# Turning the x of batches 4 and 5, the residual of batch 3 and the q and k of batch 6 by transposing transfers in a fused attention and wave-MLP kernel

## The chip, the cores and the metric

The kernel runs on one core of one Trainium2 chip. The core has five engines that run their own instruction queues and meet at semaphores: TensorE (PE in the profile, its weight loads PEld), VectorE (DVE), ScalarE (ACT), GpSimd (POOL) and SyncE (SP), which here only issues transfers. The metric is the device time of one execution in microseconds (us); smaller is better.

## The reference

Two steps on inputs of batch 8, 8 heads, 576 rows and head size 64, all float32. First, attention: a coarse one over means of four rows, repeated to full length, plus a local one in which a row sees the rows less than 4 away. Then a wave-MLP on the result, x of 576 x 512 for each batch.

```python
q_d, k_d, v_d = means of four rows of q, k, v
out_up = np.repeat(sm_attn(q_d, k_d, v_d), 4, axis=2)
mask = np.abs(pos[:, None] - pos[None, :]) < 4
out_local = softmax(where(mask, q @ k.T / 8, -1e9)) @ v
x = out_up + out_local                      # to (B, S, H * D)
theta = x @ w_theta
y = w_tok_r @ (x * cos(theta)) + w_tok_i @ (x * sin(theta))
u = x + y
return u + np.maximum(u @ w_ch, 0.0)
```

## The kernel before

Everything is computed in bf16 with sums in float32. Each batch passes through the same chain of steps, each step a small function that emits the instructions of one piece. A step has a name of two letters:

- `lk`, `lq`, `lv`, `lw` load quarters of k and q and halves of v chunks into one of 14 staging buffers `st`; `ck`, `cq`, `cv` cast them to bf16 (on DVE, ACT or POOL, as a letter says).
- `tp` turns nine 128x128 squares of q or k on TensorE into PSUM and `ev` copies them out to `kT` or `qT`. For the batches in `QKD` a transposing transfer `dk` does the turn instead, into a staging buffer, and `ev` copies from there.
- `kd`, `qd` take the means; `ps`, `ex`, `mk`, `po`, `nm` are scores, exponentials, mask, product with v and normalisation of the local part; `sd`, `ed`, `nd`, `xn`, `xd`, `xc` are the same of the coarse part (`pv`, `vd` its v); `xt` turns the local result, and `xa` adds both into `xT` (x with channels on partitions).
- `th`, `cs` are theta and its cosine and sine for 128 rows, `tt`, `ct`, `zt` the same for the last 64 rows.
- `xm` turns 128 rows of x back on TensorE into PSUM, four squares, and `zz` on DVE multiplies them with cosine and sine into `z`. For the batches in `XDMA` four transposing transfers `dx`, one for each 128 channels, fill the one buffer `xx` instead, and `zz` reads that: each `zz` needs all four `dx`, and the next batch's `dx` need all four `zz`.
- `mx` (nine products of 288 columns) mixes over rows, `ua` adds x and gives `uT`.
- `up` turns 128 rows of u back on TensorE and `uc` copies them to `ur` (the residual). For batches not in `RPE` four transposing transfers `du` fill `ur`. `zp` and `dz` are the same pair for the last 64 rows of z.
- `ch` is the product with w_ch, `rl` on DVE takes the maximum with 0 and adds `ur`, `st` stores 128 rows. `ut`, `dt`, `ht`, `rt`, `ss`, `sr` do the last 64 rows of two batches together.

Batch 0's v takes another way (`l1`, `c1`, `t1`, `e1`, `x1`). `lc`, `cc`, `la`, `ca`, `lb`, `cb`, `wp`, `wc` bring in the weights. `te` and `ts` load a table on ACT, `wm` are products on zeros that keep TensorE busy at the start.

The order of all this is a table, `ORDER`: one word for each step, with the PSUM bank, staging buffer or engine behind the name. The function `pin` ties every instruction to the one before it on its engine, so each engine runs its part of the words strictly in their order, SP's transfers included. A transfer's issue waits on SP until its source and its target are free, and everything behind it on SP waits too. Eight banks of PSUM, 14 staging buffers and five output buffers are shared by all steps.

Of the kernel before, what the change touches and what calls it, by code (L numbers as in the profile page):

```python
# [57 lines left out]
la2 cqg lb1 tp45 qdv eva wm22 tp23 eva wm65 ps67 kdg vdv lq3 qdv ckg cka ps45 cag ex wm25 sd23 ex lb4 ed cbg lk5 sd01  # L60
cqg ps67 mkv ed po45 nm po23 nd45 nd01 la6 nm la7 xn xn lk8 mkg tp23 cag po45 ex xt6 po01 cqa eva la9 lqa mkg caa xd7
lqb ckg xca ckg nm tp23 nm xt4 xt5 lbd cag lbc cbg lb2 xt7 xa cqg lb1 eva lb0 cbg lb3 lb6 tp01 xa po23 th4 xa xm5 xa
lv7 cqg nm cbg th6 lw xt7 cbg th2 lv5 xm3 evv cbg ts cs tp01 lv8 lv9 cs cbg xa tt4 zz cs xm5 wp6 wp2 zz lw lw wp3 lw
lv4 lw cbg lqa zz ct lqd eva qdg ztv wp7 cba th4 wcv zp5 lkb xm6 wcv lkc kdg wcv wp2 wp3 wcv zcv wp0 wcv wp1 cs wp7
wca wcv ps45 lk2 lk1 wcv wcv ps23 te ex qdg ps01 lq0 zz kdv cva ex mx7 mx6 mx4 cvg ua sd23 cvg cvg mkv lc3 ex po01 ua
sd67 ed ed mkv mx5 ua nm po23 ua po01 cvg pv67 nm nm mkg vda mx4 ua po23 lq6 cqg po67 nd01 nm nd45 mx2 up3 xn lq7 ckg
xn cqg lk5 cka nm tp01 xd4 lk8 up5 uca eva xcv xt3 ucv lk9 tp67 cka xt4 xt0 ua ckg xt1 kdg lv4 xa xa xa mx5 xa eva lva
tp23 ua th4 xt0 lw xa evv cqg th5 xm1 lvb lcd lqc tt0 lw lk1 lv2 lv0 lw ts cs lw xm4 cqg cs tp67 ckg cqg th2 xm3 th5
ct lw cka zz tp01 cs qdg zz cs xm2 evv ztg lc6 lc5 zp4 mx6 ccg zz qdg zcv zz eva cvg mx7 ps45 te ex ua ps23 ua ckg kdv
ex mkv ps01 mx6 lq7 mx7 po45 sd23 ex lq8 lk3 kdg ed cvg sd01 cqg ckg ua lk4 lq9 mx6 tp23 mkv lva lw lvc lw nm ua tp45  # L70
up7 cvg mkv cvv ed mx0 eva cvg pv23 ccg ua ucv eva po67 po45 ua nm up1 nm vda ccg ccg ch0 nd67 lq1 xn nd23 lkb cqg cqa
tp45 uca qdg xn mx1 xd2 xt3 eva ps67 rl lq0 ua po45 xcv kdg qdg ps01 ch2 xa ckg ex mkg nm rl mx3 ps67 cqg lv2 cka po45
ex ua sd01 lkd xt2 ckg ex nm mx3 xt4 xt5 xa up2 ua cqa cqg tp67 cvv ed up3 xa evv uca th0 xa lv6 xt1 up2 xa lw th4 xm6
ucv ts cs uca th5 cvg lq5 ckg po01 cvg zz cs nm po23 xm7 cs ch6 nm tt4 tp01 lw ct tp23 th5 rl mkg ch4 lq7 zz st eva
evv rl po67 sd01 cs cqg cvg ztg po23 ch5 nm nm rl ch4 lv8 lw te ed cvg st pv67 vda zp0 zca lk4 cka lk3 lk1 tp23 cqa
mkg ckg lq9 lqb rl qdg lva lw xm1 eva ckg utg lv0 zz lw xm5 ch4 nd67 lvc zz xn lw nd01 mx5 lvd xn mx6 st ps23 rl lv2
ua po01 kdg nm ps45 ua mx7 lk5 ex xd0 cqa xt1 ex up6 ua xcv ucv lk6 kdv tp23 cqg utg mx0 tp45 qdg xa ua eva sd67 xt2
lv8 xt3 ch1 eva xa mkg ed xa th0 mkv rl cvg lk3 lw xt6 xt7 xa xa lw lk1 cvg th2 mx1 ua ts cs xm3 cvg tt0 zz th6 st lq4
cs cvg cka po45 dt cvg ckg ct po23 th7 mx1 ztg lk7 cs lvb nm pv45 cs ckg po67 cqg kdg lw nm ua sd23 mx0 cvg nm te ed
zp1 tp67 vdv zcv ht2 tp45 xm1 rt lw ua lq9 mx3 eva zz ps67 eva ua lva qdg po45 nm ex ps01 lq0 ex xm2 up3 zz lqc nd67  # L80
uca lvd tp45 cqa xm2 qdg xn nd01 zz mx3 cka cka xn mx2 xd0 up1 lk2 lv6 kdg st ua mx3 cqa mkv lw uca xcv eva tp67 xt0
up1 lk5 ua ua cva ucv xt4 xa mx5 st xa st eva ps23 mkg sd01 qdg po67 lw ed ua nm lv3 xt4 mx5 xt6 cva mx7 po01 ua ex
sd23 xa xa po45 lw nm cvg th6 nm lq4 cqv xt0 lw ed cvv xa ts cs tp23 mkv lv8 th1 cs xm4 ua ch5 kdg lw rl ch6 lv9 eva
tt0 th1 th7 xm5 pv23 utv ct ztg zz up0 ss cqg cs zz vdv mx1 uca ua xm0 lv1 lw st zz cs tp45 lv7 cvg lv0 cvg lqb nd23
xm7 ch1 eva kdg rl nd45 xn mx0 rl xn dz ch1 sr ps23 ps45 lw lw qdg lw te ex lka zz po67 ua mx0 ex ps23 cqa ex nm rl ua
# [12 lines left out]
"""


# [1 line left out]
def kernel(  # L102
# [489 lines left out]
    def zz(b, c, w):  # L592
        x = xx[:, c, :] if b in XDMA else at.pop(("xm", b, c))
        nc.vector.tensor_tensor(out=z[b % 2][:, 2 * c:2 * c + 2, :],  # L594
# [163 lines left out]
```

## Time and profile before

| what | value |
|---|---|
| median of 3 runs | 231.97 us (231.42 to 232.17) |
| span of the profiled execution, first to last instruction | 229.4 us |
| instructions | 8506 |
| TensorE clock granted, mean | 0.996 of full |
| packets and bytes moved | 76647, 49.35 MB |
| first scores of batch 0 start at | 18.84 us |

The profile gives the execution's span, and no time of that execution beyond it; the times of the runs are from other executions. Engines work beside each other, so the sum of their busy times says nothing; what sets the time is read from where the busiest engine waits and for whom. The prediction shows the lines.

### The profile page before, as it was taken

What the parts mean: (1) busy time and instruction counts of PE and PEld (TensorE: products, weight loads), DVE (VectorE), ACT (ScalarE), POOL (GpSimd) and SP (SyncE); (2) the same over time, 40 slices, a digit from 0 to 9 for tenths busy, and PEclk for the clock granted to TensorE, in tenths of its full rate; (3) what the DMA queues carried; (4) which work ended last, traced back from release to release, by engine and by line L of the source; (5) the groups of instructions that cost most, each with busy time, mean ns of one, the idle gap of its engine ahead of it and who ended that gap; (6) DMA issues with size and microseconds to landing.
All of it is one profiled execution on the core that took longest, in us unless ns stands there. A gap on an engine that the chain in (4) does not pass through costs nothing.

```text
span 229.4 us, 8506 instructions
## 1 busy us (share of the span) xinstructions
PE 219.7 (96%) x3491; PEld 154.2 (67%) x3491; DVE 185.6 (81%) x377; ACT 159.3 (69%) x239; POOL 144.1 (63%) x190
## 2 busy tenths in 40 slices
PE   7898899999999999999999999899999999999992
PEld 2455778696778765776788667676676665677740
DVE  5168999999899899797898969979898889476382
ACT  2389899759987899689887896779879258600000
POOL 7768999929999989991984456892697310200000
PEclk9999999999999999999999999999999999999998
DMA  6999999999989999999998007996576357376677
GB/s 181 387 391 391 268 190 222 374 271 226 235 270 249 248 345 177 231 261 233 291 220 211 21 17 191 302 214 126 136 132 187 68 118 206 74 207 160 94 239 241
DMA packets 76647, 49.35 MB, mean 215 GB/s; under 512 B 61120, under 2 KB 61120, under 8 KB 76608
## 3 DMA queue, kind: packets, MB, share of 16 engines
q1 hardware_dynamic: 76608, 48.81, 83.4%
q8 instruction: 27, 0.44, 0.8%
q14 instruction: 12, 0.10, 0.1%
HBM read 33.98 MB, written 9.44 MB: 189 GB/s over the span
## 4 chain that ended last, share of the span: by engine, by line
PE 86%; DVE 7%; DMA 3%; issue 2%; SPq 1%; ACT 0%; POOL 0%; DVEq 0%
PE PS L610 30%; PE PS L548 12%; PE PS L635 12%; PE PS L304 5%; PE PS L531 4%; PE PS L512 3%; DMA st<-in_v_dram 3%; PE PS L587 2%; PE PS L483 2%; PE PS L448 2%; PE PS L560 2%; DVE tmp L521 2%; PE PS L624 2%; PE PS L652 2%; PE PS L453 1%
## 5 line engine op out<-in xcount | busy, mean ns | idle before, releaser
L610 PE MATMUL PS<-WT,z 128*128 128x288 bf16 x576 | 77.9, 286 | 0.2 <-issue 0.2
L610 PEld LDWEIGHTS <-z 128*128 128x128 bf16 x576 | 54.3, 98 | 15.8 <-issue 0.9
L615 DVE TENSOR_TENSOR uT<-PS,xT 128x288 bf16<-128x288 f32 x64 | 28.8, 452 | 11.8 <-PE PS L610 10.9
L548 PE MATMUL PS<-wth,xT 128*128 128x512 bf16 x128 | 32.2, 379 | 0.0
L635 PE MATMUL PS<-wch,uT 128*128 128x512 bf16 x128 | 31.1, 379 | 0.0
L569 POOL TENSOR_TENSOR zT<-xT,cst 128x512 bf16<-128x512 bf16 x7 | 8.1, 1153 | 34.0 <-ACT cst L566 34.0
L521 DVE TENSOR_TENSOR tmp<-PS,rl 128x512 bf16<-128x512 f32 x40 | 27.7, 692 | 1.4
L502 POOL TENSOR_TENSOR pm<-pm,band 128x1024 bf16<-128x1024 bf16 (+1 forms) x14 | 25.0, 1789 | 4.5 <-ACT pm L491 4.5
L537 DVE TENSOR_TENSOR xT<-PS,xdT 128x464 bf16<-128x464 f32 (+1 forms) x40 | 24.0, 629 | 3.0 <-ACT xdT L471 2.0
L640 DVE SCALAR_TENSOR_TENSOR osb<-PS,ur 128x512 f32<-128x512 f32 x32 | 21.8, 685 | 4.7 <-PE PS L635 4.2
L491 ACT ACTIVATE pm<-PS 128x1024 bf16<-128x1024 f32 (+1 forms) x24 | 20.4, 879 | 6.5 <-PE PS L483 6.5
L553 ACT ACTIVATE cs<-PS,pihc 128x512 bf16<-128x512 f32 x32 | 22.2, 693 | 1.6 <-PE PS L548 1.4
L720 ACT ACT_TABLE_LOAD x15 | 19.2, 1283 | 0.3
L331 POOL TENSOR_TENSOR two<-kT 128x580 f32<-128x580 bf16 x13 | 15.0, 1152 | 7.0 <-ACT kT L317 5.3
L635 PEld LDWEIGHTS <-uT 128*128 128x128 bf16 x128 | 11.9, 98 | 11.1
L554 ACT ACTIVATE cs<-PS 128x512 bf16<-128x512 f32 x32 | 19.2, 601 | 0.0
L594 DVE TENSOR_TENSOR z<-PS,cs 128x1024 bf16<-128x1024 bf16 x24 | 16.0, 682 | 2.3 <-PE PS L587 1.8
L548 PEld LDWEIGHTS <-xT 128*128 128x128 bf16 x128 | 11.3, 98 | 9.6 <-DVE xT L537 0.2
L331 POOL TENSOR_TENSOR two<-qT 128x576 f32<-128x576 bf16 x13 | 14.9, 1145 | 4.3 <-ACT qT L317 4.0
L438 ACT ACTIVATE pd<-PS 128x864 bf16<-128x864 f32 x16 | 13.8, 888 | 5.0 <-PE PS L427 4.9
L397 POOL CAST v_w<-st 128x512 bf16<-128x512 f32 x26 | 16.8, 672 | 0.0
L317 ACT COPY qT<-PS 128x1152 bf16<-128x1152 bf16 x13 | 14.6, 1121 | 2.0 <-PE PS L304 2.0
(116 smaller groups left out, 427.0 us busy)
## 6 DMA issues: line engine op xcount, KB each, us to landing
st<-in_k_dram SPq DMA_DIRECT2D x32, 288.0 KB, 6.0
st<-in_q_dram SPq DMA_DIRECT2D x32, 288.0 KB, 6.1
st<-in_v_dram SPq DMA_DIRECT2D x70, 128.0 KB, 5.2
out_dram<-osb SPq DMA_DIRECT2D x32, 256.0 KB, 2.4
st<-in_v_dram SPq DMA_DIRECT2D x4, 288.0 KB, 3.2
st<-in_moe_w_tok_r_dram SPq DMA_DIRECT2D x4, 288.0 KB, 6.5
st<-in_moe_w_tok_i_dram SPq DMA_DIRECT2D x4, 288.0 KB, 7.4
st<-in_moe_w_theta_dram SPq DMA_DIRECT2D x4, 256.0 KB, 6.3
```

The source lines that it names most:

```text
L331: nc.gpsimd.tensor_tensor(out=t, in0=src[:, :, 0:2], in1=src[:, :, 2:4], op=ALU.add)
L491: nc.scalar.activation(out=pm[(3 * b + u) % NPM][:, :, 0:n].rearrange("p e c j w -> p e (c j w)"), in_=at.pop(("ps", b, u))[:, :, 0:4 * W ...
L502: EW[w].tensor_tensor(out=t, in0=t, in1=m, op=ALU.mult)
L521: nc.vector.tensor_tensor(out=tmp[(NCH * b + c) % NTMP].rearrange("p g (j d) -> p g j d", d=D), in0=ps[:, :, :, 0:D], in1=r.unsqueeze(3).t ...
L537: nc.vector.tensor_tensor(out=xT[b % 2][:, :, CH * c:CH * c + cnt].rearrange("p e (m j) -> p e m j", j=4), in0=at.pop(("xt", b, c))[:, :, ...
L548: nc.tensor.matmul(out=ps, lhsT=xT[b % 2][:, dc, P * c:P * c + P], rhs=wth[:, dc, :], start=(dc == 0), stop=(dc == 3))
L553: nc.scalar.activation(out=t[:, 0, :], in_=ps, func=AF.Sin, bias=pihc, scale=1.0)
L554: nc.scalar.activation(out=t[:, 1, :], in_=ps, func=AF.Sin, bias=0.0, scale=1.0)
L610: nc.tensor.matmul(out=ps, lhsT=z[b % 2][:, j, P * dc:P * dc + P], rhs=WT[:, j, cols], start=(j == 0), stop=(j == 8))
L615: nc.vector.tensor_tensor(out=uT[b % 2][:, dc, cols], in0=at.pop(("mx", b, i)), in1=xT[b % 2][:, dc, cols], op=ALU.add)
L635: nc.tensor.matmul(out=ps, lhsT=uT[b % 2][:, dc, P * c:P * c + P], rhs=wch[:, dc, :], start=(dc == 0), stop=(dc == 3))
L640: nc.vector.scalar_tensor_tensor(out=o, in0=at.pop(("ch", b, c)), scalar=0.0, in1=ur[b % 2][:, c, :], op0=ALU.max, op1=ALU.add)
```

## The change

Four batches' x instead of two are turned by transfers, q and k of two batches instead of one, and the residual of five batches instead of four. The word table is another one: words now name their piece (`xt04` is chunk 4 of batch 0), so that pieces of one kind need not come in order, and nearly all banks, staging buffers and many engines of casts, copies and masks differ. The rest of the code is the same.

```diff
-XDMA = (6, 7)
+XDMA = (4, 5, 6, 7)
-RPE = (0, 1, 2, 3)
+RPE = (0, 1, 2)
 ZPE = (0, 1, 2, 3)
-QKD = (7,)
+QKD = (6, 7)
...
 ORDER = """
-l10 l11 c1g c1g k0 l12 lk3 l14 ckg c1v lk5 wm0b t101 c1g e1a kcg wm24 t123 e1a lq6 wm45 x12 cva ckg x13 cva x10 cvv
...
+l103.0 c103.g kc3.a l100.1 l101.2 kc1.a l102.3 kc2.g c100.a c101.a wm.2h t100.01 e100.v lk01.4 c102.g lk03.5 ck03.g
...
-        k0=(lambda i, w: None, span(1)), kc=(kc, span(4)), la=(la, span(4)), ca=(ca, span(4)), lb=(lb, span(9)), cb=(cb, span(9)), lc=(lc, span(4)), cc=(cc, span(4)),
+        kc=(kc, span(4)), la=(la, span(4)), ca=(ca, span(4)), lb=(lb, span(9)), cb=(cb, span(9)), lc=(lc, span(4)), cc=(cc, span(4)),
...
-    todo = {kind: iter(seq) for kind, (_, seq) in STEPS.items()}
+    todo = {(kind,) + tuple(args) for kind, (_, seq) in STEPS.items() for args in seq}
     for word in ORDER.split():
-        kind, place = word[:2], word[2:]
+        word, _, place = word.partition(".")
+        kind, args = word[:2], tuple(int(x) for x in word[2:])
...
-        STEPS[kind][0](*next(todo[kind]), place)
+        todo.remove((kind,) + args)
+        STEPS[kind][0](*args, place)
         pin()
-    for kind in todo:
-        assert next(todo[kind], None) is None, kind
+    assert not todo, todo
```

Counted from the two tables, the words that differ in number or engine:

| step | before | now |
|---|---|---|
| `tp` on TensorE / `dk` | 28 / 4 | 24 / 8 |
| `xm` / `dx` | 24 / 8 | 16 / 16 |
| `up` with `uc` / `du` | 16 / 16 | 12 / 20 |
| `wm` products | 37 | 33 |
| `cv` on POOL, ACT, DVE | 26, 7, 7 | 17, 10, 13 |
| `mk` on POOL, DVE | 14, 10 | 16, 8 |
| `kd` on POOL, DVE | 13, 3 | 15, 1 |
| `vd` on ACT, DVE | 5, 3 | 8, 0 |
| `cc` on POOL, DVE, ACT | 4, 0, 0 | 0, 3, 1 |
| `ev` on ACT, POOL, DVE | 25, 2, 5 | 21, 4, 7 |
| `te`, `ts` | 15 | 13 |

Three places of the order. The first is SP's queue behind the loads of batch 6's q and k, where `dz` of batch 4 stands before. `st_` buffers are staging, `ur` the residual, `osb` the output buffers, `xx` and `z` as above. Before (the last load for batch 6's q stands ten rows above):

```order
L288 DMA st_138<-in_q_dram 128x576
L573 DMA_TRANSPOSE z_103<-zT 128x4x128
L661 DMA out_dram<-osb_122 64x512
L349 DMA st_128<-in_v_dram 64x8x64
L349 DMA st_134<-in_v_dram 64x8x64
L349 DMA st_127<-in_v_dram 64x8x64
L288 DMA st_137<-in_k_dram 128x576
L288 DMA st_140<-in_k_dram 128x576
L288 DMA st_139<-in_q_dram 128x576
L349 DMA st_133<-in_v_dram 64x8x64
```

Of the change, from just behind the last load for batch 6's k:

```order
L340 DMA_TRANSPOSE st_135<-q_tm_77 128x9x128
L676 DMA out_dram<-osb_122 128x512
L340 DMA_TRANSPOSE st_131<-k_tm_74 128x9x128
L381 DMA st_136<-in_v_dram 64x8x64 x2
L651 DMA_TRANSPOSE ur_115<-uT_113 128x4x128
L381 DMA st_134<-in_v_dram 64x8x64
L340 DMA_TRANSPOSE st_132<-q_tm_78 128x9x128
L340 DMA_TRANSPOSE st_139<-k_tm_75 128x9x128
L651 DMA_TRANSPOSE ur_115<-uT_113 128x4x128
L676 DMA out_dram<-osb_121 128x512
L381 DMA st_138<-in_v_dram 64x8x64
L622 DMA_TRANSPOSE xx<-xT_101 128x4x128 x4
```

Where one transpose (`dz` of batch 4) stood among loads of v and of batch 7's q and k, four `dk` of batch 6, two of batch 3's `du` and the four `dx` of batch 4 now come first, and the loads for batch 7 behind them.

The second is SP's queue at the turn of batch 7's q and k. Before:

```order
L288 DMA st_131<-in_q_dram 128x576
L288 DMA st_130<-in_q_dram 128x576
L644 DMA out_dram<-osb_120 128x512
L308 DMA_TRANSPOSE st_135<-k_tm_76 128x9x128
L644 DMA out_dram<-osb_121 128x512
L308 DMA_TRANSPOSE st_138<-q_tm_79 128x9x128
L647 DMA_TRANSPOSE utr<-ut_117 128x4x128
L619 DMA_TRANSPOSE ur_114<-uT_112 128x4x128
```

Of the change:

```order
L622 DMA_TRANSPOSE xx<-xT_102 128x4x128
L320 DMA st_140<-in_k_dram 128x576
L622 DMA_TRANSPOSE xx<-xT_102 128x4x128
L320 DMA st_134<-in_q_dram 128x576
L622 DMA_TRANSPOSE xx<-xT_102 128x4x128
L320 DMA st_132<-in_q_dram 128x576
L320 DMA st_131<-in_k_dram 128x576
L622 DMA_TRANSPOSE xx<-xT_102 128x4x128
L320 DMA st_135<-in_k_dram 128x576
L340 DMA_TRANSPOSE st_139<-q_tm_77 128x9x128
```

The `dx` of batch 5 are now set between batch 7's last loads and stand ahead of its `dk`.

The third is POOL between the masks (`pm`) of batch 5 and those of batch 6. Before, with q and k of batch 6 copied out of PSUM by ACT:

```order
L502 TENSOR_TENSOR pm_86<-pm_86,band 128x1024
L331 TENSOR_TENSOR two<-qT_64 128x576
L337 TENSOR_TENSOR qd_68<-two 128x288
L397 CAST v_w_71<-st_140 128x8x64
L331 TENSOR_TENSOR two<-kT_62 128x580
L334 TENSOR_TENSOR kd_66<-two 128x2x5x29
```

Of the change:

```order
L534 TENSOR_TENSOR pm_86<-pm_86,band 128x1024
L346 COPY qT_64<-st_132 128x1152
L346 COPY kT_62<-st_131 128x2x576
L363 TENSOR_TENSOR two<-qT_64 128x576
L369 TENSOR_TENSOR qd_68<-two 128x288
L346 COPY kT_62<-st_139 128x2x576
L363 TENSOR_TENSOR two<-kT_62 128x580
L366 TENSOR_TENSOR kd_66<-two 128x2x5x29
```

POOL now copies three of batch 6's four pieces out of staging buffers, between its means.

More of the change, by code (lines that the diff above doesn't have):

```diff
@@ L61 @@
[L61 to L85, printed above, removed]
@@ new lines @@
+ex01.a mk01.v ps02.23 lk11.1 lk10.0 wm.04 sd00.01 ex02.a sd01.45 ed01.a ed00.a lk12.2 po01.67 nm01.v po00.23 nm00.v
+la3.3 ck10.g kc0.g ck11.g pv0.45 vd0.a po03.67 mk02.g po04.01 tp100.23 nd00.45 nm03.v nd01.67 ck12.a la2.5 lq13.6
+ev100.a lq12.4 cq12.g nm04.v cq13.g tp110.01 xn00.v lb4.7 cb4.g ev110.a po02.23 tp111.45 lb1.8 cb1.g ev111.a ca3.a
+xn01.v xt01.6 lb3.9 cb3.g lb0.a lb2.b nm02.v xd0.7 xc0.v xt04.0 xt00.1 la1.d xa01.v la0.0 cb0.g xt02.2 xa02.v cb2.g
+xt03.3 xa03.v lb7.1 wp6.4 ca1.a ts wc6.v wp0.5 wp4.6 wp2.7 xa04.v wc4.v lb5.4 cb5.v ca2.g ca0.g th01.2 cs01.a lq10.2
@@ new lines @@
+cb8.g th02.4 cs02.a wc0.v lb6.6 lq11.7 xm01.6 zz01.v cb7.g lq21.8 tt0.0 ct0.a cq10.g xm02.5 th03.2 cs03.a xa00.v wc2.v
+cb6.g wp1.4 th00.1 xm03.0 cq11.g lv13.9 lw13 cs00.a zz02.v wc1.v zz03.v wp7.4 tp101.23 zt0.g zp0.5 wc7.v zc0.v xm00.0
+zz00.v wp3.1 qd11.g wp5.4 wc5.v ev101.a wp8.5 wc8.v wc3.a te ps11.23 qd10.v ps10.67 ex10.a ps12.01 mx06.5 cv13.v
+lv11.a lw11 ex11.a kd10.g ex12.a lv10.b lw10 mx00.4 mx05.6 ua06.v lv14.3 kd11.g lw14 cv14.a lv12.5 sd11.57 ed11.a
+cv11.v mk10.v sd10.01 po11.23 ua00.v mk11.v mx04.4 ua05.v nm11.v ua04.v cv10.g lw12 cv12.g lq23.d ed10.a po13.67
@@ new lines @@
+nm13.v pv1.23 po10.01 nm10.v mx03.4 ua03.v vd1.a mk12.g po14.67 nm14.v lk21.0 ck21.a mx01.5 ua01.v nd10.01 lq20.c
+cq20.a xn10.v nd11.23 xn11.v lk20.1 lq30.4 cq23.g po12.45 nm12.v lk22.2 ck20.g tp200.67 ev200.a lk23.6 mx02.0 xd1.1
+xc1.v xt14.6 lq22.7 lv23.9 ck22.g xt11.7 xt12.4 ck23.g ua02.v xa14.v cq21.g tp210.23 ev210.a ts xt13.5 xa13.v xa11.v
+tp201.01 kd21.g cq22.g lv24.a lw23 tt1.6 lv21.b ct1.a up01.5 uc01.v zt1.g xt10.2 th13.3 xa12.v cs13.a xm13.5 th12.4
+ev201.v xm11.6 cs12.a qd20.g xa10.v th11.7 zz13.v lv22.3 lw22 tp211.01 ev211.v qd21.g th10.3 lk33.5 cs11.a xm10.2
@@ new lines @@
+mx15.4 lv50.2 po23.23 cq32.g cq33.a pv2.67 cc1.v ch00.5 nm23.v ua15.v lk52.0 ut1.g tp311.23 rl00.v ed21.a po24.01
+nm24.v vd2.a nd21.67 xn21.v ev311.a ch02.5 rl02.v kd30.g cv31.a ps32.01 ex32.a nd20.23 ps31.67 xn20.v xt22.4 po21.01
+ex31.a lv33.4 ch01.5 xt24.2 xd2.3 nm21.v ps30.67 ex30.a ts xt23.0 lq43.5 ck42.g mx16.1 rl01.v qd31.g xc2.v xa24.v
+lv30.b xt21.5 xa22.v lw30 cv30.g tt2.2 xa21.v ct2.a lk43.9 xa23.v xt20.6 xa20.v ck43.g tp410.34 th21.5 cs21.a mk30.g
+po30.02 lq42.7 lk40.3 ua16.v nm30.v th23.6 cs23.a th20.1 cs20.a ev410.v ck40.g lq51.6 po31.07 nm31.v lk41.a ck41.g
@@ new lines @@
+ed51.a xt44.5 mx33.1 dk600.4 xt40.0 ps50.23 sd50.67 lv64.9 lw64 xa44.v tt4.5 ex50.a xa42.v ed50.a ts cv53.g xa40.v
+du30 ht0.4 rt0.v lw51 po53.23 nm53.v th43.0 cv51.v po52.67 ct4.a mx37.4 nm52.v mk52.g ua37.v pv5.23 vd5.a th42.5
+mk50.g up21.4 po51.67 ua33.v dk611.5 ev611.g dk610.c th40.1 cs42.a uc21.a du32 ev601.a st13 nm51.v ev600.g zt4.v
+nd51.23 xn51.v lv60.b nd50.67 xn50.v qd61.g mx36.4 ua36.v ev610.g kd61.g po50.23 nm50.v th41.5 ut2.g po54.67 ch21.4
+st11 kd60.g nm54.v dx40 cs43.a dx41 xt53.0 dx42 dx43 zz43.v xd5.2 rl21.v st10 ss0 zz42.v xt51.3 up22.6 lw60 cs40.a
@@ new lines @@
+mx32.1 ch23.4 xt54.7 qd60.g uc22.v ch20.6 zz40.v cs41.a zz41.v up23.5 xc5.a dz4 ua32.v xa51.v xa54.v du33 cv64.a
+mx45.1 xa53.v uc23.a te lq73.3 xt52.5 xa52.v rl23.v lv62.1 xt50.7 lw62 ps60.23 mx40.0 xa50.v ex60.a mk60.g ch22.4
+ua45.v ua40.v lv61.0 lw61 ps61.57 rl20.v mx42.2 ua42.v ex61.a mk61.v lk70.a ck70.v lv63.6 lw63 lq72.2 st12 sd61.01
+cq73.a sd60.67 th51.5 tt5.2 ed60.a ed61.a du31 ps62.67 ex62.a ts mx44.3 cv62.v po62.01 th52.6 ua44.v cv60.v mx43.3
+mk62.g nm62.v rl22.v po60.01 nm60.v ua43.v sr0 th50.7 cs51.a cv63.g ch30.4 rl30.v dx51 cv61.g pv6.01 ct5.a zt5.v
@@ L98 @@
+mx77.6 ua77.v du73 mx73.1 ua73.v ut7.v ch63.6 rl63.v ut6.g dt3 st63 mx74.1 ua74.v du72 ch61.6 rl61.v st61 mx72.1
+ua72.v du71 ch60.6 rl60.v st60 ch62.1 rl62.v st62 ht3.2 rt3.v ss3 ch70.6 rl70.v sr3 st70 ch72.1 rl72.v st72 ch71.2
+rl71.v st71 ch73.6 rl73.v st73
 """
```

52 lines of the change are left out of this document (38 added, 14 removed).

## The prediction, made before the result

> **What bounds the kernel now.** I read the page's engine table and slices first, then the busy time by stretch, then the chain that ended last.
>
> ```profile
> PE 219.7 (96%) x3491; PEld 154.2 (67%) x3491; DVE 185.6 (81%) x377; ACT 159.3 (69%) x239; POOL 144.1 (63%) x190
> ...
> DMA  6999999999989999999998007996576357376677
> ...
> q1 hardware_dynamic: 76608, 48.81, 83.4%
> ...
> PE 86%; DVE 7%; DMA 3%; issue 2%; SPq 1%; ACT 0%; POOL 0%; DVEq 0%
> ```
>
> TensorE (PE) is busy 96% of the span and carries 86% of the chain. The DMA slices are full up to about 125 us and have a hole behind it. The stretches give the columns PE, weight loads, DVE, ACT, POOL (busy us and instructions), the granted clock, the DMA share and GB/s:
>
> ```profile
> 25.00:125.00 100.00, 99.48 (x1883) 74.92 (x1882) 90.98 (x179) 86.25 (x130) 83.57 (x106) 1.00 1.02 251
> 120.00:146.00 26.00, 26.00 (x475) 18.93 (x473) 22.34 (x46) 20.60 (x32) 13.98 (x15) 1.00 0.52 128
> 146.00:165.00 19.00, 18.06 (x244) 12.51 (x243) 15.71 (x31) 15.23 (x26) 12.98 (x15) 1.00 0.93 184
> 165.00:229.40 64.40, 59.91 (x696) 39.83 (x693) 45.66 (x90) 25.28 (x40) 15.89 (x15) 0.98 0.63 158
> ```
>
> In 25 to 125 us TensorE idles 0.5 us of 100, at clock 1.00, although the transfers are at share 1.02 there: filled rings alone do not hold it up. Every other engine has 9% or more to spare. So what counts is what TensorE no longer does, and whether something new makes it wait. The end:
>
> ```profile
> 202.80 14.33 PE PS L610 x117
> 217.14 6.91 PE PS L635 x32
> 224.04 0.88 PE PS L652 x4
> 224.94 0.69 DVE osb L656
> ```
>
> From 202.80 us TensorE never waits; after its last product at 224.92 come one DVE step and the last stores, 4.5 us (229.4 less 224.92). All sums are made against this 229.4 us span. The median of the three runs, 231.97, lies 2.57 us above it, and I keep that distance.
>
> **What leaves TensorE.** 36 transposes of `tp` (batch 6: four steps of nine), 32 of `xm` (batches 4 and 5: eight steps of four) and 16 of `up` (batch 3), 84 together.
>
> ```profile
> 32.20 0.50 PE PS L304 x9
> ...
> 83.63 0.33 PE PS L587 x4
> ...
> 91.69 0.45 PE PS L587 x8
> ...
> 135.90 0.33 PE PS L624 x4
> ```
>
> Nine in a row take 0.50 us of the chain, 0.056 each. A lone group of four shows 0.33 (0.083 each), part of it the last one's drain, under which the next group already streams; eight against four differ by 0.12 (0.03 each). The ends are so 84 x 0.03 = 2.5 us and 84 x 0.083 = 6.9 us. I take the row of nine, the longest unbroken one: 84 x 0.056 = **4.7 us** off the path. The four warm-up products fewer stand in the start, where TensorE waits for data anyway: nothing, and nothing if that cover goes, since nobody reads them.
>
> **What it puts on the transfers.** Sixteen more transposing transfers: eight `dx`, four `du`, four `dk`. Columns of the first four rows: issue time on SP's queue in ns, least, median, most; then us from issue to landing.
>
> ```profile
> L590 SPq DMA_TRANSPOSE xx<-xT x8: 1189/1264/2213, 179.1 to 199.6; - x8
> ...
> L619 SPq DMA_TRANSPOSE ur<-uT x16: 1189/1240/1832, 154.1 to 217.7; - x16
> ...
> L308 SPq DMA_TRANSPOSE st<-k_tm x2: 1318/1819/2320, 147.0 to 158.1; - x2
> L308 SPq DMA_TRANSPOSE st<-q_tm x2: 1377/1490/1602, 151.2 to 160.2; - x2
> ```
> ```profile
> ur<-uT SPq DMA_TRANSPOSE x16, 2.6
> ...
> xx<-xT SPq DMA_TRANSPOSE x8, 2.5
> ...
> st<-k_tm SPq DMA_TRANSPOSE x2, 4.5
> ```
>
> For what they take of the rings I use 205 to 220 us, where eight `ur` transfers and about four stores of 256 KB run (the first row, a stretch with `dk` in it, serves a rival below):
>
> ```profile
> 150.00:155.00 5.00, 5.00 (x86) 3.62 (x84) 3.75 (x8) 4.30 (x8) 5.00 (x6) 1.00 1.36 182
> ...
> 205.00:210.00 5.00, 5.00 (x44) 3.99 (x42) 4.16 (x9) 0.00 (x0) 0.00 (x0) 1.00 0.72 186
> 210.00:215.00 5.00, 5.00 (x43) 4.00 (x41) 1.86 (x5) 0.00 (x0) 0.00 (x0) 1.00 0.82 125
> 215.00:220.00 5.00, 5.00 (x33) 2.94 (x31) 3.10 (x7) 0.00 (x0) 0.40 (x1) 1.00 0.44 91
> 220.00:225.00 5.00, 4.91 (x23) 2.06 (x21) 3.97 (x7) 0.00 (x0) 0.00 (x0) 1.00 0.93 323
> ```
>
> The three shares from 205 us are 3.6 + 4.1 + 2.2 = 9.9 us. A store costs 0.75 us (last row: 323 GB/s at share 0.93, 0.262 MB). So a `ur` transfer of 128x512 is (9.9 - 3.0)/8 = 0.86 us of all rings, and a `dk` of 128x1152, 2.25 times that, 1.9 us. Added: 12 x 0.86 + 4 x 1.9 = 18 us on 191 (83.4% of 229.4), 209 of some 225: 93%. They fit as a whole; the hole at 125 to 136 us, where SP stood before `dz` of batch 4 (13.1 us in the row below), is what they fill.
>
> The Trainium skill (Advanced Engine Details and Errata, X-Bar Transpose (TRN2)) says that transposing transfers run as fast as plain ones, 350 to 400 GB/s. By that 128x512 in bf16 would be an estimated 0.35 us and the added load 7 us instead of 18, and the rival below would lose most of its chance. The trace disagrees with 0.86 us. The skill's VectorE: DVE Perf Modes (The three transpose paths, and its rules table) speaks against the whole change: 1309 ns by transfer against 390 ns on TensorE for one 128x128, so TensorE wherever PSUM will do. By that the 84 squares would be an estimated 110 us of transfers. The trace bears this out no better: four squares land in 2.5 us.
>
> **SP's queue.** This is the narrow place. I count the changed order from the first `dk` of batch 6 to the last of batch 7: 8 `dk`, 8 `dx`, 4 `du`, 2 `dz`, 8 loads of q and k, 11 half loads of v, 8 stores.
>
> ```profile
> 156.00 0.63 SPq L349 DMA_DIRECT2D st<-in_v_dram  x1
> ...
> 164.82 0.53 SPq L644 DMA_DIRECT2D out_dram<-osb  x1
> ...
> SPq L573 <- POOL v_w L397: 13.1, 1, 13.1
> ...
> DVE z L594 <- DMA xx<-xT: 1.2, 1, 1.2
> ...
> L594 DVE TENSOR_TENSOR z<-xx,cs 128x1024 bf16<-128x1024 bf16 x8 | 5.3, 684 | 1.2 <-DMA xx<-xT 1.2
> ```
>
> 8 x 1.65 (mean of the two `dk` medians) + 8 x 1.26 + 4 x 1.24 + 2 x 1.2 (as the others) + 27 x 0.6 = 47 us. TensorE's steps between the same points (17 `mx` at 1.10, nine of the 117 products in 14.33 us, 17 `th`, `ch` and `ht` at 0.86 = 4/32 of the 6.91 above, 14.6 us, and some 15 us of small steps, thirteen `xt` and six `nd` the largest) are 48 us. So SP has next to no slack there. Behind a late `dk` of batch 7 stand the 2.2 us evictions of its k and q on ACT and POOL, then its scores; and the half loads of v for batch 7 stand behind all of that on SP, with the DVE casts of v queued before `xa` of batch 6.
>
> For x of batch 4 the path is: last `xa`, four issues (5.0 us), 2.5 us to land, four `zz` of 0.68 (2.7 us), 10.3 us; the changed order has 15.7 us of TensorE steps between the last `xt` of batch 4 and its first `mx`. For batch 7, turned by transfers already, 12.3 us now against 14 before. Before, DVE lost 1.2 us in all waiting for `xx`. I charge **+1.2 us** for the whole of this, that same row; the ends are 0 (all covered) and what the longest issue rows give: 8 x (2.32 - 1.65) + 8 x (2.21 - 1.26) + 4 x (1.83 - 1.24) = 15 us more than 47. Some 5 us of that SP can take back by starting early, because the first `dk`'s sources are cast long before; 1 us is slack: **+9 us**.
>
> **What is moved between engines.**
>
> ```profile
> L317 ACT COPY qT<-PS 128x1152 bf16<-128x1152 bf16 x13 | 14.6, 1121 | 2.0 <-PE PS L304 2.0
> ...
> L627 ACT COPY ur<-PS 128x512 bf16<-128x512 bf16 x10 | 5.9, 589 | 5.0 <-PE PS L624 5.0
> ...
> L397 DVE CAST v_w<-st 128x512 bf16<-128x512 f32 x4 | 2.5, 623 | 0.0
> ...
> L314 POOL COPY kT<-st 128x1152 bf16<-128x1152 bf16 x1 | 2.2, 2218 | 0.0
> ```
>
> Batch 6's evictions come from SBUF: three on POOL, one on ACT, at 2.2 instead of 1.1 us. POOL so has 6.6 us more between the mask of batch 5 and the scores of batch 6's coarse part, in a stretch where it was busy 13.98 of 26 us: hidden; uncovered it would be 6.6. ACT loses four `ur` copies (2.4 us). DVE gets six casts of v (3.7 us), three of w_ch and two evictions, and gives back two masks, two k sums, three `vd` and two `ut`; net within 2 us of 185.6, with 9 free in each 100: nothing, at most +1. The start has other casts on other engines: one cast of the last q quarter earlier or later is about 1 us, and I see no sign: 0, ends -1 and +1. At the end, fewer `ch` steps stand between the last `mx` and the first use of batch 7's residual: 0, at most +1.
>
> **Sum.** 229.4 - 4.7 + 1.2 = 225.9 us of span, 228.5 us of time. I say **228.4 us**.
>
> **Rivals.**
> *SP's queue becomes the bound* (slower). Place: from the first `dk` of batch 6 to the v loads of batch 7. Price: +9 - 4.7, so 236 us, 232.7 to 240 with part of it. It decides once the issues there take over about 53 us. For it: SP's sum is 47 against 48, the rings are at 1.36 in the worst 5 us with `dk` before. Against it: at share 1.02 TensorE idled 0.5 of 100 us.
> *The gain turns into waits*: TensorE arrives sooner at steps whose partner on DVE or ACT is no sooner (DVE was busy 90.98 of 100). Price: what is saved, about 4.5 us back, so 231.8 us. Against it: 9% of DVE is free.
> *More than the sum*: the upper price of a transpose (6.9) and a start 1 us shorter with no waits, 224.1 to 226.
>
> **Chances.** Forecast 0.58 (its own range 226 to 231), SP's queue 0.24, gain turned into waits 0.12 (0.02 faster, 0.07 same, 0.03 slower), more than the sum 0.06. Within 0.3% (231.3 to 232.7) counts as no change, about what a measurement here can tell apart. Faster 0.58 + 0.06 + 0.02 = 0.66, same 0.07, slower 0.27. The range 225.2 to 235 leaves out about half of the second case and a little of the last.
>
> **What would show it.** Right: PE's busy time down by about 4.7 us, idle time between 25 us and the end within 2 us of before, `xx` now waited for at three or four places, DMA share near 1 from 105 to 165 us with the hole gone, POOL's three 2.2 us copies with TensorE busy beside them. Wrong: DVE waiting for `xx`, or TensorE or its weight loads waiting for kT or qT from SBUF copies, or for v_w of batch 7, for several us; issue times of transposes on SP over 2 us; slices of PE under 9 between 110 and 175 us. If PE's busy time falls less than 2.5 us, the price of a transpose is wrong.

## The result, and the profile after

The changed kernel takes 249.16 us (median of four runs, 246.76 to 249.65) against 231.69 (230.16 to 232.17) for the kernel before: ratio 1.074, 95% interval 1.068 to 1.080. It is 17.5 us slower where I forecast 3.6 us faster, and lies far outside my range. The span of its profiled execution is 247.1 us, 17.7 more than before.

The page after: engine table, slices, transfer queue, chain of waits by engine.

```profile
PE 223.1 (90%) x3373; PEld 153.8 (62%) x3403; DVE 193.4 (78%) x377; ACT 157.0 (64%) x241; POOL 150.2 (61%) x183
...
PEclk9999799999999997999999999999999999999999
DMA  7999999992299995577999867999888577767667
...
q1 hardware_dynamic: 87872, 51.56, 84.5%
...
PE 64%; DVE 16%; ACT 5%; DMA 5%; issue 4%; POOL 2%; SPq 1%; DVEq 0%; ACTq 0%; POOLq 0%
```

The rings did what was forecast: 84.5% of 247.1 is 209 us, the very sum. But TensorE's share of the chain fell from 86% to 64%, DVE's rose from 7 to 16. No other engine is fuller than before; they are late one after another. By stretch, after (PE, PEld, DVE, ACT, POOL busy; clock; DMA share; GB/s):

```profile
25.00:125.00 100.00, 94.79 (x1632) 70.96 (x1641) 88.78 (x168) 77.25 (x120) 76.21 (x92) 0.97 0.86 219
66.00:95.00 29.00, 24.65 (x435) 17.65 (x437) 23.86 (x45) 19.60 (x31) 24.23 (x29) 0.96 1.02 245
100.00:144.00 44.00, 43.69 (x814) 31.07 (x816) 37.56 (x76) 35.98 (x59) 34.49 (x36) 1.00 0.91 187
144.00:192.00 48.00, 41.81 (x645) 28.16 (x651) 37.63 (x72) 33.32 (x46) 33.79 (x32) 1.00 0.89 190
...
25.00:225.00 200.00, 186.90 (x2963) 132.20 (x2988) 167.26 (x320) 140.25 (x215) 132.53 (x143) 0.98 0.86 197
```

Before, the last of these stretches and the second:

```profile
25.00:225.00 200.00, 198.46 (x3183) 141.96 (x3179) 169.59 (x336) 144.12 (x220) 124.53 (x147) 1.00 0.83 201
66.00:95.00 29.00, 28.76 (x528) 20.27 (x526) 26.19 (x52) 25.34 (x40) 27.33 (x35) 1.00 0.98 247
```

From 25 to 225 us TensorE idles 13.1 us instead of 1.5, and in the 29 us from 66 every engine does less: 435 products on TensorE instead of 528. The idle time lies in two stretches, ahead of 100 us and behind 144; between them TensorE idles 0.3 us of 44. In neither is it one wait. The waits of TensorE after, longest first (total, times, longest):

```profile
PE PS L642 <- DVE uT L647: 3.3, 3, 1.4
PE PS L619 <- DVE tmp L553: 2.0, 1, 2.0
PE PS L642 <- DVE xdn L491: 1.8, 1, 1.8
PE PS L667 <- DVE osb L672: 1.7, 2, 1.1
...
PE PS L592 <- DVE tmp L553: 1.0, 1, 1.0
```

To see where it collects, I add up the work of TensorE's steps in their order (`mx` 1.10 us, `th` and `ch` 0.86, `tp` 0.50 and so on, as in the prediction) and subtract that sum from the moment at which each step starts. What is left is the time by which TensorE is behind its own work so far: idle time, what it lost at half clock (3.4 us in all after the change, see the end), and short groups that take longer. It works out as (us; columns e9 and e18 are runs below):

| work done | before | after | e9 | e18 |
|---|---|---|---|---|
| 20 | 8.9 | 11.0 | 10.3 | 8.1 |
| 50 | 9.4 | 12.6 | 12.4 | 10.0 |
| 70 | 10.1 | 16.4 | 16.3 | 11.4 |
| 100 | 10.7 | 22.3 | 19.4 | 13.3 |
| 130 | 10.7 | 26.2 | 23.4 | 15.2 |
| 170 | 12.4 | 32.7 | 28.0 | 19.7 |
| 200 | 12.5 | 34.1 | 32.4 | 22.6 |

The work itself fell by 5.5 us (206.6 against 212.1), and 21.6 more is lost. More than half of that, 11.6 us, is lost by 122 us (100 of work and 22.3). There the first added transfer is only being issued. The issues of `dk` after (ns least, median, most; first and last start):

```profile
L340 SPq DMA_TRANSPOSE st<-q_tm x4: 1244/1400/2905, 121.8 to 172.3; - x4
L340 SPq DMA_TRANSPOSE st<-k_tm x4: 1286/1348/2705, 125.4 to 174.4; - x4
```

So the transfers, on which I spent most of the prediction, cannot be the cause of that half. It is in the rest of the table: the new sequence and its engines. For the other half that is less plain: the added pieces take part in it (the slow `zz` below), but e4, a run below without any of them, idles 6.6 us of the 56 from 144 to 200 us all the same. The end is 1.5 us longer too (the last four `rl` wait for the residual):

```profile
240.58 2.52 DVE L672 SCALAR_TENSOR_TENSOR osb<-PS,ur 128x512 f32<-128x512 f32 x4 [1.89 <-DMA ur<-uT]
```

### The profile page after: what moved, and what is told of

It is laid out like the page before. It is cut to its first block, busy times and chain, and to the rows that moved or that the text cites. A ratio compares the mean times of both kernels' runs of the same rounds, so it can differ in the third digit from the quotient of the medians.

```text
span 247.1 us, 8277 instructions
## 1 busy us (share of the span) xinstructions
PE 223.1 (90%) x3373; PEld 153.8 (62%) x3403; DVE 193.4 (78%) x377; ACT 157.0 (64%) x241; POOL 150.2 (61%) x183
## 3 DMA queue, kind: packets, MB, share of 16 engines
q1 hardware_dynamic: 87872, 51.56, 84.5%
## 4 chain that ended last, share of the span: by engine, by line
PE 64%; DVE 16%; ACT 5%; DMA 5%; issue 4%; POOL 2%; SPq 1%; DVEq 0%; ACTq 0%; POOLq 0%
PE PS L642 23%; PE PS L580 7%; PE PS L667 7%; PE PS L336 5%; DVE z L626 4%; PE PS L544 3%; PE PS L563 3%; PE PS L748 2%; DMA out_dram<-osb 2%; PE PS L515 2%; DVE osb L672 2%; DVE xT L569 2%; DVE uT L647 2%; DVE tmp L553 2%; PE PS L480 2%
## 5 line engine op out<-in xcount | busy, mean ns | idle before, releaser
L642 PE MATMUL PS<-WT,z 128*128 128x288 bf16 x576 | 78.8, 286 | 5.2 <-DVE uT L647 3.3
L647 DVE TENSOR_TENSOR uT<-PS,xT 128x288 bf16<-128x288 f32 x64 | 28.4, 452 | 15.8 <-PE PS L642 13.1
L534 POOL TENSOR_TENSOR pm<-pm,band 128x512 bf16<-128x512 bf16 (+1 forms) x16 | 26.2, 1637 | 13.5 <-ACT pm L523 9.9
L580 PE MATMUL PS<-wth,xT 128*128 128x512 bf16 x115 | 31.1, 381 | 1.2 <-issue 0.6
L585 ACT ACTIVATE cs<-PS,pihc 128x512 bf16<-128x512 f32 x32 | 22.3, 697 | 11.2 <-PE PS L580 10.9
L672 DVE SCALAR_TENSOR_TENSOR osb<-PS,ur 128x512 f32<-128x512 f32 x32 | 21.6, 683 | 7.7 <-PE PS L667 3.2
L363 POOL TENSOR_TENSOR two<-kT 128x580 f32<-128x580 bf16 x15 | 18.6, 1238 | 10.7 <-ACT kT L349 5.8
L667 PEld LDWEIGHTS <-uT 128*128 128x128 bf16 x128 | 11.9, 99 | 13.3 <-issue 3.2
L601 POOL TENSOR_TENSOR zT<-xT,cst 128x512 bf16<-128x512 bf16 x6 | 6.9, 1153 | 21.0 <-DVE xT L569 16.3
L586 ACT ACTIVATE cs<-PS 128x512 bf16<-128x512 f32 x32 | 19.4, 607 | 0.0
L363 POOL TENSOR_TENSOR two<-qT 128x576 f32<-128x576 bf16 x13 | 15.9, 1224 | 2.3 <-ACT qT L349 2.0
L580 PEld LDWEIGHTS <-xT 128*128 128x128 bf16 x128 | 10.9, 98 | 10.0 <-issue 1.1
L349 ACT COPY kT<-PS 128x1152 bf16<-128x1152 bf16 x9 | 10.0, 1118 | 10.6 <-PE PS L336 10.6
L329 POOL CAST k_tm<-st 128x576 bf16<-128x576 f32 x22 | 15.2, 702 | 1.0 <-DMA st<-in_k_dram 0.7
L329 POOL CAST q_tm<-st 128x576 bf16<-128x576 f32 x20 | 13.4, 676 | 3.9 <-DMA st<-in_q_dram 3.9
```

The source lines that it names most:

```text
L329: COPY[w](out=to[:, r, :], in_=of[:, r, :])
L363: nc.gpsimd.tensor_tensor(out=t, in0=src[:, :, 0:2], in1=src[:, :, 2:4], op=ALU.add)
L534: EW[w].tensor_tensor(out=t, in0=t, in1=m, op=ALU.mult)
L580: nc.tensor.matmul(out=ps, lhsT=xT[b % 2][:, dc, P * c:P * c + P], rhs=wth[:, dc, :], start=(dc == 0), stop=(dc == 3))
L585: nc.scalar.activation(out=t[:, 0, :], in_=ps, func=AF.Sin, bias=pihc, scale=1.0)
L642: nc.tensor.matmul(out=ps, lhsT=z[b % 2][:, j, P * dc:P * dc + P], rhs=WT[:, j, cols], start=(j == 0), stop=(j == 8))
```

## The experiments

"Old order" is the kernel before with the transfers set into its own table, "new order" the changed kernel. All times in us; the ratio is the measured one to the kernel before on the same chip (its medians 230.6 to 231.7; a quotient of medians can differ from it by up to 0.3%).

| run | time | ratio, 95% interval |
|---|---|---|
| the change itself | 249.16 | 1.074 (1.068 to 1.080) |
| e1 old order, x | 246.18 | 1.066 (1.061 to 1.071) |
| e2 old order, q and k | 234.16 | 1.013 (1.008 to 1.018) |
| e3 old order, all three | 252.07 | 1.090 (1.085 to 1.096) |
| e4 new order, no added transfer | 258.24 | 1.116 (1.110 to 1.123) |
| e5 old order, new engines | 260.69 | 1.129 (1.122 to 1.137) |
| e6 new order, old engines | 272.34 | 1.178 (1.170 to 1.185) |
| e7 new order, cv22 earlier | 247.96 | 1.073 (1.066 to 1.080) |
| e8 old order, x set later | 238.10 | 1.030 (1.024 to 1.035) |
| e9 new order, neighbouring banks | 246.56 | 1.064 (1.059 to 1.069) |
| e10 new order, x on TensorE | 250.08 | 1.083 (1.078 to 1.088) |
| e11 new order, q, k on TensorE | 252.52 | 1.091 (1.085 to 1.097) |
| e12 old order, residual | 237.10 | 1.025 (1.021 to 1.028) |
| e13 old order, residual set later | 234.37 | 1.014 (1.010 to 1.018) |
| e14 old order, no masks | 230.53 | 0.998 (0.995 to 1.001) |
| e15 new order, no masks | 242.76 | 1.050 (1.045 to 1.055) |
| e16 new order, one sine | 247.74 | 1.071 (1.066 to 1.075) |
| e17 old order, residual, mended | 231.56 | 1.002 (0.999 to 1.005) |
| e18 new order, light | 239.85 | 1.035 (1.030 to 1.040) |

**Transfers or order? e1 to e4.** The transfers alone in the old table, and the new table without them:

```diff
+XDMA = (4, 5, 6, 7)
...
 cv54.v xa44
+dx40 dx41 dx42 dx43
 ts cs40
...
 ck73.g xa54
+dx50 dx51 dx52 dx53
 xn60
```

That is e1, with `zz` of batches 4 and 5 some steps later. e2 sets `dk600.3`, `dk601.9`, `dk611.c` and `dk610.7` behind the casts of their sources and `lq63`, `cq63` earlier; e3 is e1, e2 and e12 (below) together. e4 takes the transfers out of the new table:

```diff
 cs43.a
-dx41
+xm43.6
 xt53.0
...
 zz43.v
+xm42.7
 xd5.2
...
 ua25.v
+tp600.67
 lv51.7
```

and so on for all 84, with `ev6` and `uc3` on ACT.

> The kernel before, in its own order, with x of batches 4 and 5 alone turned by transposing transfers (eight dx, their zz set some steps later). Theory T, the transposing transfers cost the time (rings and SP's queue, and what reads them late): 235 to 239 us. Theory O, the new order with its engine places is what costs, and the transfers are as good as hidden: 232.0 less 32 x 0.056, 229 to 231 us, no more than 1 us of idle time of TensorE more than before.

> The kernel before, in its own order, with q and k of batch 6 alone turned by four transposing transfers; their evictions stay where the order had them, but now read SBUF. Theory T: 234 to 238 us, the stand at the evictions of 2.2 us. Theory O: 232.0 less 36 x 0.056, 229 to 231 us.

> The kernel before, in its own order, with all three sets of transposes (84) on transfers. Theory T: it is as slow as the change or worse, 244 to 255 us. Theory O: 232.0 less 4.7, 226 to 230 us. In between, 232 to 242: both matter.

> The changed kernel in its new order and with its new engines, but with the 84 transposes back on TensorE (xm of batches 4 and 5, up of batch 3, tp of batch 6, these with their evictions on ACT). Theory T: back to 231 to 236 us. Theory O: it stays slow, 247 to 255 us (249 plus up to 4.7).

Both theories failed in part: e2 and e3 came out as theory T has it, e1 and e4 above both ranges. The new order without a single added transfer is the slowest of these four, 26.8 us over the kernel before (11.6% of 231): the order costs, and the transfers take part of it back. In e4 the stretch from 66 to 95 us reads as it does after the change:

```profile
66.00:95.00 29.00, 24.76 (x435) 17.30 (x433) 23.45 (x44) 19.16 (x31) 24.01 (x29) 0.96 1.01 243
```

(I set e4's transposes in by hand, so 26.8 may hold some cost of my own.) But in the old order the transfers cost 15, 3 and 21 us as I had placed them. The waits of SP's queue in e1 say why:

```profile
SPq L620 <- DVE uT L645: 14.8, 1, 14.8
...
SPq L620 <- DVE xdn L489: 4.2, 1, 4.2
SPq L620 <- DVE rl L550: 4.1, 1, 4.1
```

L620 is `dx`. SP reached the first one 14.8 us before its source was done: the last `xa` of batch 4 ends at 131.41 us, and `dx` is issued at 131.43. What stood behind it came late: loads of v and q, for which POOL and ACT then waited (3.8 us the longest), and the `dz` of batches 4 and 5, whose target TensorE's `mx` reads. TensorE's longest waits in e1 are for these two:

```profile
PE PS L640 <- DMA z<-zT: 8.4, 2, 5.0
```

In the kernel before it never waited for that transfer. During the second of the two waits its clock also fell to half, for 6.8 us in which it was busy 3.9. In e2 POOL waited for a late load of v, though TensorE's own longest wait behind the start is 1.1 us there:

```profile
POOL v_w L427 <- DMA st<-in_v_dram: 9.0, 1, 9.0
```

**Is it the place in SP's queue? e8, e12, e13, e17.** The same transfers where SP stands idle:

```diff
 rl22 xn51
+dx40 dx41 dx42 dx43
 dz4
+zz40 zz41 zz42
 ch23.1
...
 dk711.9
+dx50 dx51 dx52 dx53
 mx46.3
```

is e8. For the residual of batch 3, e12 sets `du30` to `du33` behind `ua31`, `ua33`, `ua35` and `ua37`, e13 and e17 as here (e13 with `du33` behind `lq73.3` instead):

```diff
 rl22 xn51
+du30 du31 du32
 dz4
...
 cv62.g lv71.6
+du33
 mx42.1
```

> As the first run, x of batches 4 and 5 by transfers in the old order, but its eight dx stand where SP gets to them when their source is ready (those of batch 4 just before dz of batch 4, where SP stands anyway; those of batch 5 behind the last dk of batch 7). Theory P, the first run lost by where they stood in SP's queue, the loads behind them late: 230 to 234 us. Theory T, the transfers themselves cost it: 240 to 247 us.

> The kernel before, in its own order, with the residual of batch 3 alone turned by four transfers, each behind the ua that ends its source. Theory P, only a transfer whose reader is near costs time, and this one's reader is tens of us away: 229 to 231.5 us (16 x 0.056 less TensorE work). Theory T, each transfer at its head holds SP's queue and costs: 233 us or more.

> The kernel before in its own order, residual of batch 3 by four transfers as in run e12, but three of them stand just before dz of batch 4, where SP stands some 12 us in any case, and the fourth behind the last q load of batch 7. Theory P, a transfer costs by what it holds up behind it in SP's queue: 229 to 231.5 us. Theory T, the transfers themselves cost: 235 us or more.

> As run e13, but the fourth transfer of the residual of batch 3 stands some thirty steps earlier, behind the second v load of batch 7 and ahead of the first step that reads it; in e13 it stood behind that reader, and SP stood 5.2 us before it. Theory P, a transfer costs by what it holds up in SP's queue: 229.5 to 232 us. Theory T, it costs wherever it stands: 233.5 us or more.

In e13 the last transfer stood behind the first `rl` that reads it, so one block took an old quarter and SP stood before it. The four transfers of the residual cost 5.7 us (2.5%; theory T), 3.2 (between the theories) and then 0.4 (theory P), the last within the bound of no change. Waits of SP for `uT` before `du`, in e12:

```profile
SPq L649 <- DVE uT L645: 16.5, 8, 9.2
```

and in e17:

```profile
SPq L648 <- DVE uT L644: 8.6, 8, 1.9
```

Longest stand 9.2 against 1.9 us. So the four transfers of the residual cost by what they hold up, not in themselves. But e17 gains nothing either, although 16 transposes left TensorE (0.9 us by my price). And for x the place is only part of it: e8 lies between its two theories and still loses 3% (6.8 us). There the transfers' own path is too long. Between the last `xa` and the first `mx` of batch 5 stand some 9 us of TensorE's work, for a path that the prediction put at 10.3, and in e8 the wait goes through from `xx` to TensorE:

```profile
DVE z L624 <- DMA xx<-xT: 4.6, 2, 3.2
...
PE PS L640 <- DVE z L624: 4.3, 3, 2.8
```

From 171.1 to 177.9 us TensorE then runs at half clock, busy for 5.5 us, so another 2.8 us of work are lost.

**Sequence or engines? e5, e6.**

```diff
-cv22.g
+cv22.v
...
-cc0.g
+cc0.v
...
-mk21.v
+mk21.g
...
```

These are three of e5's changes; e6 does the reverse in the new table.

> The kernel before: its sequence of steps and its transposes on TensorE, but with the changed kernel's engine for each of the some 120 casts, copies, masks and sums that change engine (the evictions of batch 6 stay on ACT). Theory E, the new engine places cost the time (casts from SBUF on DVE beside a busy POOL take longer): 240 us or more. Theory S, the new sequence costs it and the engines do not matter: 230 to 234 us.

> The changed kernel with its own sequence and its transposing transfers, but with the engines of the kernel before for the same some 120 steps (the evictions of batch 6 stay as changed). Theory E: 232 to 241 us. Theory S: 247 us or more, since the sequence is tuned to its own engines.

Theory E held in e5, theory S in e6. The new sequence with the old engines (e6) is 24 us worse than with its own (the change). The old sequence with the new engines and no added transfer (e5) is 3 us worse than the new sequence with them (e4), the intervals just overlapping. So neither half is cheap without the other, and how much of the loss each makes is not shown: a table's sequence and engines are one schedule. What can be read is how sensitive such a table is: some 120 letters, with DVE's busy time up by 5.6 us (185.6 to 191.2) and ACT's by 3.8, cost 29.9 us.

**A load that SP holds up? e7.** After the change SP stood 6.2 us before a load of w_ch, and the transfers have a hole at 55 to 68 us. The first row is from SP's waits, the second from the stretch:

```profile
SPq L273 <- DVE uT L647: 6.2, 1, 6.2
```
```profile
55.00:68.00 13.00, 12.02 (x205) 8.79 (x203) 12.27 (x18) 12.27 (x22) 12.53 (x13) 1.00 0.27 70
```

```diff
 ev211.v
+cv22.v
...
 ut0.v
-cv22.v
```

> The changed kernel with one cast of v of batch 2 (cv22) some thirty steps earlier in DVE's queue, so that the staging slot for which SP stands 6.2 us at 58 to 64 us comes free sooner; nothing else. Theory H, the hole in the transfers there makes the loss of 66 to 95 us: 242 to 246 us. Theory D, DVE's and ACT's own lateness makes it: 248 to 250 us.

In e7 the stand before w_ch is at most 2.6 us and the DMA share from 55 to 68 us is 0.60, but the ratio is that of the change: the hole is not the cause.

**False waits. e9.** The new table gives ten steps two PSUM banks that are not neighbours; the old one has none. A read of banks 0 and 7 is tracked as a read of everything between, so a step on bank 5 waits for it. The semaphore counts of the built program show seven such waits, three of TensorE and four of DVE, none before. The worst, `xm21` on bank 5 behind the read of banks 0 and 7 (`nm31`), after the change:

```profile
89.27 0.32 PE L544 MATMUL PS<-v_w,pm 64*64 64x65 bf16 x16
91.57 0.40 PE L619 MATMUL PS<-ident,xT 128*128 128x128 bf16 x4 [1.98 <-DVE tmp L553]
```

```diff
-po30.02 th23.6 po31.07 xm21.5 po61.17 tt6.4 xt61.7 sd11.57 sd71.13 ps72.47 mx51.3
+po30.67 th23.2 po31.56 xm21.7 po61.45 tt6.7 xt61.4 sd11.23 sd71.34 ps72.34 mx51.7
```

> The changed kernel with other PSUM banks for eleven steps, so that po30, po31, po61, sd11, sd71 and ps72 take two neighbouring banks. As it stands, a read of two banks that are not neighbours (0 and 7, say) makes steps that use a bank between them wait, though they share nothing with it: three such waits of TensorE and four of DVE, none in the kernel before. Theory F: these waits (2.0 us before xm21, about 1 before tt6, 0.5 before th20, 1.1 and 1.3 on DVE) and the half clock behind the longest (1.7 us) are a fair part of the loss: 243 to 246.5 us. Theory L, the steps behind them are late anyway: 248 to 250 us.

e9 so mends six of the ten. The same two steps in e9:

```profile
88.87 0.32 PE L544 MATMUL PS<-v_w,pm 64*64 64x65 bf16 x16
89.12 0.40 PE L619 MATMUL PS<-ident,xT 128*128 128x128 bf16 x4
```

The wait is gone, and 1% with it (2.3 us; 1.074 to 1.064, the intervals just overlapping; 246.56 lies just above the range of theory F). So the false waits taken away are some seventh of the loss. By the table above e9 is 4.7 us ahead of the change at 170 of work and 1.7 at 200; of those 3.0 us, 1.7 went at half clock (204.2 to 207.6 us in e9).

**Do the transfers pay in the new order? e10, e11.**

e10 holds the `xm` and e11 the `tp` of e4, each alone:

```diff
-XDMA = (4, 5, 6, 7)
+XDMA = (6, 7)
```
```diff
-QKD = (6, 7)
+QKD = (7,)
```

> The changed kernel with x of batches 4 and 5 alone back on TensorE (xm beside the zz, 32 transposes, 1.8 us), everything else as changed. Theory Z, the zz of these batches, read from SBUF beside a busy POOL (up to 1.6 us each instead of 0.68), and SP's queue cost more than the transposes: 242 to 248 us. Theory G, in the new order the transfers of x are a gain: 250 to 254 us.

> The changed kernel with q and k of batch 6 alone back on TensorE (36 transposes, 2.0 us) and their four evictions of 1.1 us on ACT from PSUM in place of 2.2 us on POOL and ACT from SBUF. Theory Q, the copies of 2.2 us make batch 6 late and are a cause of the loss: 243 to 248 us. Theory G, in the new order these transfers are a gain: 250 to 254 us.

Theory G held twice, for x by a hair. For q and k the transfers pay, for x probably: without them it is 1.7% and 0.9% slower (3.9 and 2.0 us; the interval of the second overlaps that of the change). My price for the same transposes was 2.0 and 1.8.

**Who is late? e14, e15, e16, e18.**

The first line is left out in e14, e15 and e18, the second in e16 and e18; e18 also has the banks of e9:

```diff
-        EW[w].tensor_tensor(out=t, in0=t, in1=m, op=ALU.mult)
...
-        nc.scalar.activation(out=t[:, 1, :], in_=ps, func=AF.Sin, bias=0.0, scale=1.0)
```

> The kernel before without its band masks on the scores (24 multiplications, some 26 us of POOL and 10 of DVE are left out; the scores go on unmasked). Theory W, the changed kernel loses its time to TensorE's waits for late DVE, POOL and ACT steps, the kernel before to TensorE's own work: this one gains little, 228 to 231 us. Theory V, both wait alike: it gains as much as the changed one does.

> The changed kernel without its band masks on the scores (24 multiplications on POOL and DVE left out). Theory W: 236 to 243 us, since the steps that wait for masked scores and for what is queued behind masks on DVE and POOL come sooner. Theory A, it is ACT (sines, exponentials) that is late: 246 to 249 us.

> The changed kernel without the second of the two sines of each full token block (32 ACT steps of 0.59 us left out, 19 us; their place in cs holds a constant). Theory A, ACT's lateness holds TensorE: 236 to 243 us. Theory W with DVE and POOL as the late ones: 245 to 249 us.

> The changed kernel with the neighbouring banks of e9 and, left out, the masks (as e15) and the second sine of each full block (as e16): all the lateness of DVE, POOL and ACT that these runs can take away, at once. Theory W, TensorE's waits on the other engines are the loss: 232 to 238 us. Theory R, something else of the new order (transfers late, TensorE's own steps) holds it as well: 239 us or more. Summed from the single runs: 249.2 - 2.6 - 6.4 - 1.4 = 238.8.

Without the masks the old order gains nothing that can be told from none; the new one gains 2.4% (5.6 us). This is the clearest sign of the difference: the old order hides the masks whole, the new one does not. The second sine gives at most 0.4%, its interval overlapping that of the change. With masks, sine and banks together 3.5% are left, 8 us, so theory R held: something else is late as well. TensorE from 25 to 225 us in e18:

```profile
25.00:225.00 200.00, 194.85 (x3034) 135.81 (x3034) 162.12 (x324) 125.62 (x183) 103.09 (x125) 1.00 0.92 206
```

It idles 5.2 us here (in the fastest execution of e18, 237.27 us) against 13.1, so more than half of the idle time there came from the three. What makes the rest, spread over many waits of 0.3 to 1.6 us on DVE and ACT, stays open.

No run that keeps all steps beats the kernel before; e17 equals it.

## Why the prediction was wrong

**The step that failed** is the one on the moves between engines: "net within 2 us of 185.6, with 9 free in each 100: nothing, at most +1". I compared sums of busy time. The sum itself was too small: DVE is busy 193.4 us after the change, 7.8 more (4.0 of it the slow `zz` below), and 5.6 more in e5, where nothing but the engines changed. But the main fault is to read a sum as cover. In a table where every engine runs strictly in order, a sum says nothing of when an instruction is done; what counts is how far ahead of its reader it is. I priced the words that the diff names (the transfers) one by one and the some 1200 that it re-orders by one sentence. e4, with all those words and none of the added transfers, is 26.8 us slower, against the at most 1 us that I gave the moves. Which of the words are the late ones stays open beyond masks, second sine and banks (e18).

**The rival of the right kind was capped.** "The gain turns into waits" was priced at "what is saved, about 4.5 us back". Nothing limits waits to what was saved: 21.6 us more is lost.

**TensorE's 84 transposes:** -4.7 us; the work did fall (5.5 by the step sum). PE's busy time, my sign for it, rose by 3.4 all the same. So it is no measure of the work: 6.8 us ran at half clock, which is 3.4 us more, and short groups are recorded as busy for longer (the same 640 `po` products 12.2 us instead of 10.9), in part at half clock. Set back in the new order the transposes cost 9.7 us together (e4 against the change, 4.2%), twice my price: there TensorE waits as well, and my splice is in it.

**The rings:** right, 209 us, but not full.

**x by transfers, +1.2 us:** after the change `zz` never waited for `xx`; 0 would have been right. The path was covered there, and in e8 it was not. What I missed sits in `zz`. I took 0.68 us from a row of the kernel before in which POOL stood idle. After (columns: ns least, median, most; first and last start):

```profile
L626 DVE TENSOR_TENSOR z<-PS,cs x16: 675/686/692, 33.8 to 123.0; 128x1024 bf16<-128x1024 bf16 x16
L626 DVE TENSOR_TENSOR z<-xx,cs x16: 678/682/2659, 148.2 to 222.8; 128x1024 bf16<-128x1024 bf16 x16
```

One `zz` took 2.66 us. DVE's timeline there, then POOL's:

```profile
172.46 3.26 DVE L626 TENSOR_TENSOR z<-xx,cs 128x1024 bf16<-128x1024 bf16 x2
```
```profile
172.94 2.23 POOL L346 COPY kT<-st 128x1152 bf16<-128x1152 bf16 x1 [3.77 <-DMA st<-k_tm]
```

The second of the two `zz` starts at 173.06, behind the start of POOL's copy, and ends at 175.72, 0.55 us behind the copy's end: it waited for the copy and then ran. Behind it TensorE waits 1.8 us (the `xdn` row among the waits). From PSUM no `zz` took over 0.69, with POOL busy beside most of them. The Trainium skill (SBUF, Who interferes with whom) has the rule: a DVE instruction with two SBUF inputs contends with a GpSimd instruction that reads SBUF, and whoever comes second is blocked whole. At 173 us the trace agrees. At 177.3 us it was POOL that paid: two `zz` took 0.68 each, and the `qd` of POOL beside them 2.32 instead of 0.67, although it is recorded as the one that started first. The change made both halves: `zz` with two SBUF inputs and copies of 2.2 us on POOL. In all DVE was busy 14.6 us with the 16 `zz` from `xx`, instead of 10.6 (twice the 5.3 of the eight before). These 4.0 us are not the main part, and taking away either half (e10, e11) gained nothing.

**SP's queue as the bound:** not after the change. Its stands were short and e7 shows that the longest costs nothing. The mechanism is real, as e1 and e12 show in the old order, but the new order had set its transfers where they hold up little.

**The start**, 0 with ends of 1, was +2.1, of which 1.7 is a stretch at half clock (below). **The end**, 0 to +1, was +1.5.

## What to carry to other kernels

When a change replaces a whole hand-written order, price the order first, and do not read free shares of busy time as cover. What could be counted instead is how many microseconds of the bounding engine's work lie between each producer and its reader; no run here has tried that as a forecast. Price a transfer by what stands behind it in its queue, and put it where the queue stands anyway (5.7 us against none for the same four transfers). A step that is moved from PSUM to SBUF must be priced beside what POOL does at that moment. A two-bank PSUM piece should take neighbouring banks (2.0 us of one wait went with them).
